# Attention block with a token-mixing MLP on one core: the last heads' repeated rows loaded first, half a row tile more in the last pair, no maximum tiles in the first iteration

## The chip, the cores and the metric

The kernel runs on one core of a Trainium2 chip. The metric is the device time of one execution in microseconds (us); a version of the kernel is given by the median of several executions. The engines of the core work side by side and are tied together by semaphores: TensorE (PE) multiplies matrices, VectorE (DVE) and ScalarE (ACT) do elementwise work and empty the accumulators (PSUM banks), GpSimd (POOL) helps with elementwise work, and the SP queue issues most loads and stores. ACT and POOL issue a few DMAs as well.

## What is computed

`x` is a sequence of 2048 tokens of width 640. Two branches read it, and a gate of each token mixes them:

```python
qkv = (x @ wqkv).reshape(B, S, 3, H, Dh).transpose(2, 0, 3, 1, 4)    # H = 32 heads of Dh = 20
q, k, v = qkv
p = softmax(einsum("bhqd,bhkd->bhqk", q, k) * Dh ** -0.5)
a = einsum("bhqk,bhkd->bhqd", p, v).transpose(0, 2, 1, 3).reshape(B, S, D) @ wo

h = layernorm(x)                                                     # over the channels
u = gelu(einsum("bsd,sf->bdf", h, w1) + b1)                          # F = 1728, over the tokens
b = (einsum("bdf,fs->bds", u, w2) + b2).transpose(0, 2, 1)

g = sigmoid((x * gate_w).sum(-1, keepdims=True))
out = g * a + (1 - g) * b
```

All of it is float32. The kernel keeps the accuracy by splitting operands into a high and a low part and multiplying three times (high x high, high x low, low x high).

## The kernel before

**Stages.** First come the projections to q, k and v, and the layer norm. Then comes the MLP, whose result, already weighted by 1 - g, is stored to DRAM as `y_d`. During the MLP the maxima that the softmax needs are computed for the first half of the head pairs. Then comes the attention loop, and behind it the product with `wo`, here called the tail.

**The attention loop** runs over 16 pairs of heads (`p`) and 32 iterations (`it`) in each: two halves of the queries by 16 tiles of keys. One iteration does this on PE: two score matmuls into a double bank (`st_pair`, one wide exponential on ACT), a third score matmul into a single bank (`st_one(g, 0)`), then up to two maximum tiles, a fourth score matmul (`st_one(g, 1)`), and eight `pv` matmuls of the iteration before, which need its exponentials. The single score tiles rotate over the banks `one0`, `one1` and `s3`. A *maximum tile* (`s_next`, line 213) is a score matmul into one of two `s` banks whose rows DVE reduces to their maxima (line 219); they are made ahead of their use, for later head pairs. `LEFT` of them are left for the loop, and `take` says how many an iteration does: two in each iteration but the very first, until they run out. That is in iteration 8 of the last pair. The very first iteration of the first pair has its scores made ahead, so the first one that computes scores is number 1.

**The last pair.** When the maximum tiles have run out, the `s` banks are free, and the last pair does part of the tail's work between its scores. `first_row` and `row_half` multiply the first row tile (128 tokens, the first 512 of 640 input channels) by `wo`, in two halves of 320 output columns; a pass is a pair of matmuls on 64 rows each (`pair64`, line 49), and a half has 12 passes. A half uses both `s` banks and is emptied by two DVE instructions that add it to the row of `y_d` loaded before (line 1057).

**What hangs on the last pv.** The output of the heads `o_d`, not yet divided by the sums `l_d`, goes through DRAM. For the early heads the reciprocals are repeated for each of the 20 channels of a head in `r_d`. For the last four heads that is done behind the loop: `last_load` loads their sums, `last_recip` takes the reciprocals on DVE and stores them to `rc_d` from ACT's queue, and `l_rest` loads each row of `rc_d` 20 times, into 20 partitions of the tile `rbl` (four DMAs of 160 KB, line 1011).

**The tail.** Its operands are loaded in two kinds of tiles. *e-tiles* (`e_load(q)`, q = 0 to 7) hold the first 512 channels for 256 tokens: 512 KB of `o_d` (`ore`) and 512 KB of reciprocals (`rbe`). The *l tile* (`l_load`) holds the last 128 channels for all tokens: 1 MB of `o_d` (`orl`), 384 KB of `r_d` for the heads before the last four (into partitions 0 to 47 of `rbl`), and the rows from `l_rest` in the others. `e_high` and `l_high` multiply output by reciprocal on DVE (line 978) and take the high part on ACT (line 980); `e_low` and `l_low` take the low part on DVE (line 986). Row tiles then go through `a_tile` (line 1142): tile t needs the e-tile t // 2, and for its last 128 channels the l tile. Tiles 1 to 7 do only the first 512 channels at first. Tiles 8 to 15 do all of them, and each is followed by the missing part of tile t - 8. The results rotate over four pairs of banks, and an evacuation on DVE (line 1148) adds each to the row of `y_d`; then it is stored.

**What sets the order.** In this part the order of every engine's instructions and of the SP queue is the order in which the program writes them. So a DMA on SP that waits holds up all that SP issues later, and a DVE instruction that waits for a load holds up the evacuations behind it. Before the change SP issues e4, l, e5, then the repeated rows, then e6 and e7. On DVE, the multiplication of e5 is written in tile 4's turn ahead of the evacuation of tile 4, that of l in tile 6's turn.

Of the kernel before, what the change touches and what calls it, by code (L numbers as in the profile page):

```python
# [7 lines left out]
F32 = mybir.dt.float32  # L8
F32R = mybir.dt.float32r
AF = mybir.ActivationFunctionType  # L10
OP = mybir.AluOpType
AX = mybir.AxisListType

P = 128
S, D, H, DH, F = 2048, 640, 32, 20, 1728
NP = H // 2
NT = S // P
NC = D // P
# [6 lines left out]
HALF = D // 2  # L25
# [6 lines left out]
def gated_mix(ctx, tc, xT, x, wqk, wv0, wv1, wo, w1, w1t, b1, w2, b2, out):  # L32
    nc = tc.nc
# [29 lines left out]
    o_d = dram.tile([D, S], F32, name="o_d")  # L63
# [8 lines left out]
    psum = ctx.enter_context(tc.tile_pool(name="psum", bufs=1, space=PSUM))  # L72
# [19 lines left out]
    def s_tile(shape, name):  # L92
        return psum.tile(shape, F32, tag="s", bufs=2, name=name)
# [22 lines left out]
    g_t = cp.tile([P, NT], F32, name="g_t")  # L116
# [324 lines left out]
    for half in range(2):  # L441
        wvh, wvl = wvs[half]
        width = HALF + 2 if half == 0 else HALF
        for t in range(NT):
            n = NT * half + t
# [11 lines left out]
            ps = one_tile([P, width], f"v{half}_{t}")  # L457
            q, cols = t // 4, slice((t % 4) * P, (t % 4 + 1) * P)
# [387 lines left out]
    ap = ctx.enter_context(tc.tile_pool(name="ap", bufs=1))  # L846
# [89 lines left out]
    woh = [ap.tile([P, D], F32R, name=f"woh{c}") for c in range(NC)]  # L936
# [8 lines left out]
    o_raw, o_hl, l_hl = {}, {}, {}  # L945
# [13 lines left out]
    tys = {}  # L959
# [28 lines left out]
    def e_load(q):  # L988
        o_load(q, slice(0, (NC - 1) * P), NC - 1, 256, "e", 2)
# [6 lines left out]

    L0 = (H - LAST) * DH - (NC - 1) * P

    def l_load():
        raw, rb = [ap.tile([P, 4, 512], F32, name=f"{n}l") for n in ("or", "rb")]  # L1000
        r0 = (NC - 1) * P
        nc.sync.dma_start(raw.rearrange("p a b -> p (a b)"), o_d[r0:])
        rb = rb.rearrange("p a b -> p (a b)")
        nc.sync.dma_start(rb[:L0], r_v[r0:r0 + L0])
        for q in range(4):
            o_raw[q, "l"] = raw[:, q:q + 1], rb[:, q * 512:(q + 1) * 512].unsqueeze(1)
        return rb

    def l_rest(rb):
        for h in range(LAST):  # L1010
            nc.sync.dma_start(rb[L0 + h * DH:L0 + (h + 1) * DH], rc_d[h:h + 1].broadcast_to([DH, S]))
# [24 lines left out]

    def st_one(g, j):
        n = (2 * g + j) % 3
        ps = psum.tile([P, 512], F32, tag=("one0", "one1", "s3")[n], bufs=1, name=f"st{g}_1{j}")
        st_mm(g, j, 1, ps)  # L1040
        pt = lp.tile([P, 512], F32, tag="pt", bufs=5, name=f"p{g}_1{j}")
        nc.scalar.activation(pt, ps, AF.Exp, scale=SCALE)  # L1042
        pts[g][j, 1] = pt

    row_mms, row_ps, row_evacs = [], [], []

    def row_half(c):
        row_ps[:] = [s_tile([P, HALF], f"a0_{c}_{k}") for k in range(2)]
        oh, ol = o_hl[0]
        cols = slice(c * HALF, (c + 1) * HALF)  # L1050
        passes = [e for k in range(NC - 1) for e in ((oh[:, k, :P], woh[k]), (oh[:, k, :P], wol[k]), (ol[:, k, :P], woh[k]))]
        for i, (a, b) in enumerate(passes):
            row_mms.append((list(row_ps), a, b[:, cols], i == 0, i == len(passes) - 1))

        def evac(ps=list(row_ps)):
            for k in range(2):
                nc.vector.scalar_tensor_tensor(tys[0][:, cols], ps[k], g_t[:, :1], tys[0][:, cols], op0=OP.mult, op1=OP.add)

        row_evacs.append(evac)

    def first_row(it):
        if it in (10, 21):
            row_half(it // 21)
        for _ in range(2 if it in (14, 18, 26) else 1):
            if row_mms:
                pair64(*row_mms.pop(0))
        if it == 19:
            row_evacs.pop(0)()

    LEFT = NP * 128 + 2 - S_AHEAD  # L1070
    for p in range(NP):
        qs = st_src[p][1]
        if 8 <= p < 8 + NC:
            load_wo(p - 8)
        for it in range(32):
            qh, kt = divmod(it, NT)
            if p + 1 < NP:
                if it == 6:
                    st_src[p + 1] = base_stack(p + 1, True)
                if it == 13:  # L1080
                    load_v(p + 1)
                if it == 27:
                    load_m(p + 1, st_src[p + 1][1], 0)
            if it == 12 and p:
                load_m(p, qs, 1)
            if it == 14 and due_stack:
                n = due_stack.pop()
                if n < NP:
                    s_src[n] = s_stack(n)
            if p == NP - 1:  # L1090
                if it in (0, 14, 18, 29):
                    e_load((0, 14, 18, 29).index(it))
                if 13 <= it < 13 + NT:
                    y_load(it - 13)
                if it in (5, 20, 25):
                    q = (5, 20, 25).index(it)
                    e_high(q, lp if q == 2 else ap, nc.gpsimd)
                    e_low(q, nc.gpsimd)
            if kt == 0:
                pv = psum.tile([P, 512], F32, tag="pv", bufs=1, name=f"pv{p}_{qh}")  # L1100
            take = min(LEFT - given, 2) if p or it else 0
            g = p * 32 + it
            if g:
                st_pair(g)
                if p == NP - 1:
                    first_row(it)
                st_one(g, 0)
            else:
                pts[0] = first_p
            for _ in range(take):  # L1110
                s_next()
            if g:
                st_one(g, 1)
            given += take
            if take and given == LEFT:
                s_finish()
            pv_flush()
            if p * 32 + it in later:
                later.pop(p * 32 + it)()
            pend.append((p, qh, kt, pv, pts.pop(p * 32 + it)))  # L1120
    def a_tile(t, cs):
        n = a_count[0] % 4
        a_count[0] += 1
        name = f"a{t}_{cs[0]}"
        if n == 0:
            two = psum.tile([P, 2, 512], F32, tag="two", bufs=1, name=name)
            ps = [two[:, i, :HALF] for i in range(2)]
        elif n == 2:
            ps = [s_tile([P, HALF], f"{name}_{i}") for i in range(2)]
        else:  # L1130
            ps = [psum.tile([P, HALF], F32, tag=tag, bufs=1, name=f"{name}_{tag}") for tag in (("one1", "one0") if n == 1 else ("s3", "pv"))]
        passes = []
        for k in cs:
            (oh, ol), n, i = (o_hl[t // 2], 2, k) if k < NC - 1 else (l_hl[t // 4], 4, 0)
            cc = slice((t % n) * P, (t % n + 1) * P)
            passes += [(oh[:, i, cc], woh[k]), (oh[:, i, cc], wol[k]), (ol[:, i, cc], woh[k])]
        mms = [(i, c) for i in range(len(passes)) for c in range(2)]
        if t == NT - 1:
            mms.sort(key=lambda e: e[1])
        for i, c in mms:  # L1140
            a, b = passes[i]
            nc.tensor.matmul(ps[c], a, b[:, c * HALF:(c + 1) * HALF], start=(i == 0),  # L1142
                             stop=(i == len(passes) - 1))

        def evac():
            c = slice(t, t + 1)
            for i in range(2):
                nc.vector.scalar_tensor_tensor(tys[t][:, i * HALF:(i + 1) * HALF], ps[i], g_t[:, c], tys[t][:, i * HALF:(i + 1) * HALF], op0=OP.mult, op1=OP.add)
                if t == NT - 1:
                    put = (nc.scalar if i else nc.sync).dma_start  # L1150
                    put(out[t * P:(t + 1) * P, i * HALF:(i + 1) * HALF], tys[t][:, i * HALF:(i + 1) * HALF])
            if t != NT - 1 and NC - 1 in cs:
                nc.sync.dma_start(out[t * P:(t + 1) * P, :], tys[t])

        return evac

    a_count = [0]
    assert not row_mms
    first = a_tile(1, range(NC - 1))
    row_evacs.pop(0)()  # L1160
    first()
    pv_flush()
    e_load(4)
    last_rb = l_load()
    e_high(3, lp)
    e_low(3)
    e_load(5)
    last_recip()
    l_rest(last_rb)
    for t in range(2, NT):  # L1170
        q = t // 2 + 3
        lates = {NT // 2 - 2: (2, 0), NT // 2 + 1: (3, 1)}.get(t, ())
        for n in lates:
            l_high(n)
        for n in lates:
            l_low(n)
        if t % 2 == 0 and q < NT // 2:
            e_high(q, ap if q % 4 < 2 else lp)
        evacs = [(t, range(NC) if t >= NT // 2 else range(NC - 1))]
        if t >= NT // 2:  # L1180
            evacs.append((t - NT // 2, [NC - 1]))
        if t == NT - 1:
            evacs.reverse()
        evacs = [a_tile(*e) for e in evacs]
        for f in evacs:
            f()
        if t % 2 == 0 and q < NT // 2:
            e_low(q)
            if q + 2 < NT // 2:
                e_load(q + 2)  # L1190
# [49 lines left out]
```

## Time and profile before

| | us |
|---|---|
| median of 3 runs (lowest to highest) | 1772.01 (1771.06 to 1773.87) |
| the profiled execution's own time | 1770.92 |
| its span, first to last instruction | 1769.1 |
| first scores of the loop to the last pv, about | 723.4 to 1698.5 |
| the tail behind it | 1698.5 to 1769.1 |
| PE busy | 1760.1 (99%) |
| ACT busy | 1482.0 (84%) |
| DVE busy | 1225.9 (69%) |
| POOL busy | 659.9 (37%) |

TensorE's granted clock was 1.00 in all of the span. A busy PE includes the time of pipelined matmuls, so two engines can both read as busy all the time while one of them sets the pace. In the profile's rows the first number is the start in us from the span's beginning, the second the length; what stands in square brackets is the idle time ahead of the instruction on its engine, and what ended it. `SPq` and `ACTq` are DMA issues of these queues. Names such as `st`, `pv`, `ore`, `rbl` are the program's tiles; the tiles of the row product are called `a`, `a_one`, `a_s` and `a_pv` after the banks that they use.

### The profile page before, as it was taken

How to read it: one execution, taken by the hardware profiler on the slowest of the kernel's cores; microseconds unless marked ns; L12 is line 12 of the kernel's file. 1: busy time of each engine (PE TensorE's matmuls, PEld its weight loads, DVE VectorE, ACT ScalarE, POOL GpSimd, SP SyncE). 2: the span in 40 equal slices, each digit the busy share in tenths (PEclk: the TensorE clock that was granted, in tenths of full speed). 3: DMA queues.
4: the chain of work that ended last, by engine and by line, in shares of the span. 5: the costliest groups of instructions: out<-in, count | busy, mean ns of one | idle time of the engine just before them, and what ended most of it. 6: DMA issues, size and time to landing. Idle time of an engine off the chain costs nothing.

```text
span 1769.1 us, 39556 instructions
## 1 busy us (share of the span) xinstructions
PE 1760.1 (99%) x15008; PEld 1091.6 (62%) x15008; DVE 1225.9 (69%) x2379; ACT 1482.0 (84%) x2565; POOL 659.9 (37%) x988
## 2 busy tenths in 40 slices
PE   9999999999999999999999999999999999999998
PEld 7998899999999999533333333333333333333378
DVE  5303289999999899776777676777777677767335
ACT  4354388888888886899999999999999999999930
POOL 2223577889877777111211111121322121211400
PEclk9999999999999999999999999999999999999999
DMA  8767876467675564434314234053353143301553
GB/s 304 248 196 252 266 184 172 142 176 208 179 200 144 156 187 138 101 63 110 65 41 86 49 73 94 10 114 67 49 140 73 43 94 66 73 19 45 195 136 137
DMA packets 155625, 225.20 MB, mean 127 GB/s; under 512 B 66548, under 2 KB 93572, under 8 KB 151752
## 3 DMA queue, kind: packets, MB, share of 16 engines
q1 hardware_dynamic: 136902, 193.14, 40.1%
q0 software_dynamic: 15648, 24.28, 5.8%
q10 hardware_dynamic: 2884, 5.25, 1.1%
q8 instruction: 118, 1.93, 0.5%
q14 instruction: 73, 0.60, 0.1%
HBM read 166.88 MB, written 55.36 MB: 126 GB/s over the span
## 4 chain that ended last, share of the span: by engine, by line
PE 97%; DMA 2%; DVE 1%; ACT 0%; issue 0%; SPq 0%; ACTq 0%; DVEq 0%
PE pv L931 29%; PE st L1027 23%; PE s L213 12%; PE y L49 10%; PE u L49 10%; PE qk L55 8%; PE v L55 4%; PE a_one L1142 1%; PE a L1142 1%; DMA rc_d<-rl_last 1%; DMA ore<-o_d 0%; PE a_pv L1142 0%; PE a_s L1142 0%; DMA k_d<-evh 0%; DMA wr<-in_wqk_dram 0%; PE a L49 0%
## 5 line engine op out<-in xcount | busy, mean ns | idle before, releaser
L219 DVE TENSOR_REDUCE mx<-s 128x1 f32<-128x512 f32 x1280 | 835.2, 687 | 280.9 <-PE s L213 143.7
L1042 ACT ACTIVATE p<-st 128x512 f32<-128x512 f32 x1022 | 563.4, 618 | 0.0
L931 PE MATMUL pv<-p,v 128*32 128x512 f32 x4088 | 545.3, 605 | 0.0
L1034 ACT ACTIVATE p<-st 128x1024 f32<-128x1024 f32 x511 | 532.7, 1042 | 1.5 <-PE st L1027 1.4
L1027 PEld LDWEIGHTS st<-qs_True,ks_True 62*128 62x128 f32 x2044 | 245.1, 185 | 433.8 <-ACT p L1034 425.9
L1027 PE MATMUL st<-qs_True,ks_True 62*128 62x512 f32 x2044 | 494.6, 446 | 0.1
L213 PE MATMUL s<-ks_False,qs_False 60*128 60x512 f32 x1152 | 325.1, 391 | 0.4 <-ACT ov L228 0.3
L44 POOL TENSOR_TENSOR wl<-wr,wh 128x512 fp32r<-128x512 f32 x228 | 275.5, 1220 | 62.5 <-ACT wh L41 49.1
L238 DVE CUSTOM_DVE_ANT_0 ov<-s,ov 128x512 f32<-128x512 f32 x384 | 264.1, 688 | 36.2 <-PE s L213 24.7
L213 PE MATMUL s<-sk,sq 60*128 60x512 f32 x896 | 281.6, 394 | 0.0
L228 ACT ACTIVATE ov<-s 128x512 f32<-128x512 f32 x384 | 228.8, 598 | 63.0 <-PE s L213 53.0
L912 POOL DMA_DIRECT2D l_d<-oev x124 | 60.7, 496 | 411.0 <-DVE oev L904 402.6
L49 PE MATMUL y<-gh,wh 64*128 64x320 f32 x896 | 198.2, 305 | 0.0
L213 PEld LDWEIGHTS s<-ks_False,qs_False 60*128 60x128 f32 x1152 | 194.5, 184 | 3.1 <-ACT ov L228 0.9
L931 PEld LDWEIGHTS pv<-p,v 128*32 128x32 f32 x4088 | 81.3, 108 | 186.1 <-issue 174.5
L49 PE MATMUL u<-hh,wh 64*128 64x320 f32 x864 | 192.9, 304 | 0.0
L49 PE MATMUL u<-hl,wh 64*128 64x320 f32 x864 | 192.8, 304 | 0.0
L49 PE MATMUL y<-gh,wl 64*128 64x320 f32 x832 | 191.8, 305 | 0.0
L49 PE MATMUL y<-gl,wh 64*128 64x320 f32 x832 | 191.6, 305 | 0.0
L49 PE MATMUL u<-hh,wl 64*128 64x320 f32 x800 | 180.9, 304 | 0.0
L41 ACT ACTIVATE wh<-wr 128x512 fp32r<-128x512 f32 (+3 forms) x247 | 146.9, 599 | 38.3 <-PE y L49 15.7
L213 PEld LDWEIGHTS s<-sk,sq 60*128 60x128 f32 x896 | 166.2, 186 | 15.2 <-DVE mx L219 0.4
(189 smaller groups left out, 2388.8 us busy)
## 6 DMA issues: line engine op xcount, KB each, us to landing
wr<-in_w_dram SPq DMA_DIRECT2D x192, 256.0 KB
ks_True<-k_d SPq DMA_DIRECT2D x96, 160.0 KB
qs_True<-q_d SPq DMA_DIRECT2D x192, 80.0 KB
qs_False<-q_d SPq DMA_DIRECT2D x96, 80.0 KB
v_d<-vt SPq DMA_DIRECT2D x32, 212.0 KB
sk<-k_d SPq DMA_DIRECT2D x42, 160.0 KB
sq<-q_d SPq DMA_DIRECT2D x84, 80.0 KB
v<-v_d SPq DMA_DIRECT2D x15, 424.0 KB
```

The costliest lines, as they stand in the source:

```text
L41: nc.scalar.activation(hi, src, AF.Copy)
L44: (lo_eng or nc.vector).tensor_sub(lo, src, hi.bitcast(F32))
L49: nc.tensor.matmul(ps[k], a[r], b[r], start=start, stop=stop)
L55: nc.tensor.matmul(ps, a, b, start=(i == 0 and k == 0), stop=(i == n - 1 and k == 2))
L213: nc.tensor.matmul(ps, qs[half][r, t * P:(t + 1) * P], ks[r, kc * 512:(kc + 1) * 512], start=True, stop=True)
L219: nc.vector.tensor_reduce(mx[:, slot, j, t: t + 1], ps, axis=AX.X, op=OP.max)
L228: nc.scalar.activation(over[j, kc], ps, AF.Relu)
L238: nc.vector.tensor_tensor_reduce(ov, ps, ov, 1.0, -3.0e38, OP.add, OP.max, mx[:, slot, j, t: t + 1])
L931: nc.tensor.matmul(pv[r: r + 32, :], v_tiles[p][:, kt, VW * j: VW * j + 32], pt[j, c], start=(kt == 0), stop=(kt == NT - 1))
L1027: nc.tensor.matmul(ps, ks[r, kt * P:(kt + 1) * P], qs[qh][r, c * 512:(c + 1) * 512], start=True, stop=True)
L1034: nc.scalar.activation(pt, ps, AF.Exp, scale=SCALE)
L1042: nc.scalar.activation(pt, ps, AF.Exp, scale=SCALE)
```

## The change

Three things are edited.

The loads of the tail: the l tile's buffers are made ahead without a load (`l_tiles`), the reciprocals and the four loads of repeated rows come directly behind e4, and the l tile's own loads and e5 come behind them. The multiplication of the first l tiles moves from tile 6's turn to tile 5's.

The row product in the last pair: three halves instead of two (row tile 0 whole, and the first 320 columns of row tile 1), begun in iterations 10, 18 and 26, with two passes in an iteration except in 15, 16, 23 and 24. Behind the loop only the other half of tile 1 is left, and the third half's evacuation.

The loop's first iteration does no maximum tiles, so all of them come one iteration later and the last two fall into iteration 9 of the last pair. The fourth score tile of that first iteration goes to an `s` bank instead of `one0`.

```diff
+    l_raw = []
+
+    def l_tiles():
+        raw, rb = l_raw[:] = [ap.tile([P, 4, 512], F32, name=f"{n}l") for n in ("or", "rb")]
+        for q in range(4):
+            o_raw[q, "l"] = raw[:, q:q + 1], rb[:, q:q + 1]
+        return rb.rearrange("p a b -> p (a b)")
+
     def l_load():
-        raw, rb = [ap.tile([P, 4, 512], F32, name=f"{n}l") for n in ("or", "rb")]
         r0 = (NC - 1) * P
-        nc.sync.dma_start(raw.rearrange("p a b -> p (a b)"), o_d[r0:])
-        rb = rb.rearrange("p a b -> p (a b)")
+        raw, rb = [t.rearrange("p a b -> p (a b)") for t in l_raw]
+        nc.sync.dma_start(raw, o_d[r0:])
         nc.sync.dma_start(rb[:L0], r_v[r0:r0 + L0])
-        for q in range(4):
-            o_raw[q, "l"] = raw[:, q:q + 1], rb[:, q * 512:(q + 1) * 512].unsqueeze(1)
-        return rb
...
     def st_one(g, j):
         n = (2 * g + j) % 3
-        ps = psum.tile([P, 512], F32, tag=("one0", "one1", "s3")[n], bufs=1, name=f"st{g}_1{j}")
+        if (g, j) == (1, 1):
+            ps = s_tile([P, 512], f"st{g}_1{j}")
+        else:
+            ps = psum.tile([P, 512], F32, tag=("one0", "one1", "s3")[n], bufs=1, name=f"st{g}_1{j}")
...
     def first_row(it):
-        if it in (10, 21):
-            row_half(it // 21)
-        for _ in range(2 if it in (14, 18, 26) else 1):
+        if it in (10, 18, 26):
+            n = (10, 18, 26).index(it)
+            row_half(n // 2, n % 2)
+        for _ in range(1 if it in (15, 16, 23, 24) else 2):
             if row_mms:
                 pair64(*row_mms.pop(0))
-        if it == 19:
+        if it in (16, 24):
             row_evacs.pop(0)()
...
-            take = min(LEFT - given, 2) if p or it else 0
+            take = min(LEFT - given, 2) if p or it > 1 else 0
...
-    first = a_tile(1, range(NC - 1))
+    first = a_tile(1, range(NC - 1), (1,))
     row_evacs.pop(0)()
     first()
     pv_flush()
     e_load(4)
-    last_rb = l_load()
+    last_rb = l_tiles()
     e_high(3, lp)
     e_low(3)
-    e_load(5)
     last_recip()
     l_rest(last_rb)
+    l_load()
+    e_load(5)
     for t in range(2, NT):
         q = t // 2 + 3
-        lates = {NT // 2 - 2: (2, 0), NT // 2 + 1: (3, 1)}.get(t, ())
+        lates = {NT // 2 - 3: (2, 0), NT // 2 + 1: (3, 1)}.get(t, ())
```

`row_half` now takes the row tile as well as the half, and `a_tile` takes the halves that it computes and empties.

More of the change, by code (lines that the diff above doesn't have):

```diff
@@ L1045, in gated_mix, with row_half @@
     row_mms, row_ps, row_evacs = [], [], []
-    def row_half(c):
-        row_ps[:] = [s_tile([P, HALF], f"a0_{c}_{k}") for k in range(2)]
+    def row_half(t, c):
+        row_ps[:] = [s_tile([P, HALF], f"a{t}_{c}_{k}") for k in range(2)]
         oh, ol = o_hl[0]
+        rows = slice(t * P, (t + 1) * P)
         cols = slice(c * HALF, (c + 1) * HALF)
-        passes = [e for k in range(NC - 1) for e in ((oh[:, k, :P], woh[k]), (oh[:, k, :P], wol[k]), (ol[:, k, :P], woh[k]))]
+        passes = [e for k in range(NC - 1) for e in ((oh[:, k, rows], woh[k]), (oh[:, k, rows], wol[k]), (ol[:, k, rows], woh[k]))]
         for i, (a, b) in enumerate(passes):
@@ L1056, in evac @@
             for k in range(2):
-                nc.vector.scalar_tensor_tensor(tys[0][:, cols], ps[k], g_t[:, :1], tys[0][:, cols], op0=OP.mult, op1=OP.add)
+                nc.vector.scalar_tensor_tensor(tys[t][:, cols], ps[k], g_t[:, t:t + 1], tys[t][:, cols], op0=OP.mult, op1=OP.add)
         row_evacs.append(evac)
     def first_row(it):
-        if it in (10, 21):
-            row_half(it // 21)
-        for _ in range(2 if it in (14, 18, 26) else 1):
+        if it in (10, 18, 26):
+            n = (10, 18, 26).index(it)
+            row_half(n // 2, n % 2)
+        for _ in range(1 if it in (15, 16, 23, 24) else 2):
             if row_mms:
                 pair64(*row_mms.pop(0))
-        if it == 19:
+        if it in (16, 24):
             row_evacs.pop(0)()
@@ L1120, in gated_mix, with a_tile @@
             pend.append((p, qh, kt, pv, pts.pop(p * 32 + it)))
-    def a_tile(t, cs):
+    def a_tile(t, cs, halves=(0, 1)):
         n = a_count[0] % 4
@@ L1136, in a_tile @@
             passes += [(oh[:, i, cc], woh[k]), (oh[:, i, cc], wol[k]), (ol[:, i, cc], woh[k])]
-        mms = [(i, c) for i in range(len(passes)) for c in range(2)]
+        mms = [(i, c) for i in range(len(passes)) for c in halves]
         if t == NT - 1:
@@ L1146, in evac @@
             c = slice(t, t + 1)
-            for i in range(2):
+            for i in halves:
                 nc.vector.scalar_tensor_tensor(tys[t][:, i * HALF:(i + 1) * HALF], ps[i], g_t[:, c], tys[t][:, i * HALF:(i + 1) * HALF], op0=OP.mult, op1=OP.add)
```

## Prediction

> **What bounds the kernel now.** I read the chain of waits first, by its shares and then in order of time, then the timelines of TensorE (PE), ScalarE (ACT), VectorE (DVE) and the SP queue around the three places that the diff touches: the start of the attention loop, its last pair, and the stage behind it. All times are of the profiled execution.
>
> The shares of the chain:
>
> ```profile
> PE 97%; DMA 2%; DVE 1%; ACT 0%; issue 0%; SPq 0%; ACTq 0%; DVEq 0%
> ```
>
> The end of the same chain (start, length, what ran):
>
> ```profile
> 1693.76 3.72 PE a L1142 x24
> 1697.48 1.07 PE pv L931 x8
> ...
> 1701.32 1.86 DMA rl_last<-l_d
> 1703.79 9.69 DMA rc_d<-rl_last
> ```
>
> The reader sees that PE sets the time nearly everywhere, and that the one long exception lies in the tail: 32 KB of reciprocals of the last heads need 9.69 us to reach DRAM, and their repeated rows (rbl) can be loaded only then. In the loop, PE and ACT both run without a gap at about 1.90 us an iteration, so small things decide there which of them is late.
>
> **First iteration without maximum tiles.** ACT's exponentials at the loop's start, and the two rows that made the second one late:
>
> ```profile
> 724.01 1.02 ACT L1034 ACTIVATE p<-st 128x1024 f32<-128x1024 f32 x1 [1.07 <-PE st L1027]
> 724.93 1.08 ACT L1042 ACTIVATE p<-st 128x512 f32<-128x512 f32 x2
> 726.33 1.03 ACT L1034 ACTIVATE p<-st 128x1024 f32<-128x1024 f32 x1 [0.32 <-PE st L1027]
> ...
> 728.23 1.02 ACT L1034 ACTIVATE p<-st 128x1024 f32<-128x1024 f32 x1
> ```
>
> ```profile
> 723.71 0.61 DVE L708 TENSOR_SCALAR ty<-y,omg,b2o 128x320 f32<-128x320 f32 x1 [3.64 <-PE y L49]
> ```
>
> ```profile
> 724.37 0.49 PE L1027 MATMUL st<-qs_True,ks_True 62*128 62x512 f32 x1
> ```
>
> The wide exponentials start 2.32 us apart, then 1.90: 0.42 us are lost once. The fourth score matmul (724.37) sat behind two maximum tiles and waited for DVE to empty bank one0 (723.71 + 0.61 = 724.32). The change takes away both: no maximum tiles, and this matmul writes to an s bank. At most 0.42 us is gained. But the next iteration's second maximum tile rotates onto that s bank and must wait for the exponential reading it, which ends at 724.93 + 1.08 = 726.0, about 0.4 us after PE would reach the tile; part of the gain goes back. I take **-0.2** (bounds -0.42 and 0). The two tiles reappear in iteration 9 of the last pair, which now has none. ACT sets the period there, so they cost nothing in themselves; but they leave ACT with no backlog for what follows.
>
> **Half a row tile more in the last pair.** PE with two row pairs in an iteration, then with one (starts of the first score matmuls of three iterations), and ACT's wide exponentials:
>
> ```profile
> 1659.55 0.50 PE L1027 MATMUL st<-qs_True,ks_True 62*128 62x512 f32 x2
> ...
> 1661.52 0.50 PE L1027 MATMUL st<-qs_True,ks_True 62*128 62x512 f32 x2
> ...
> 1663.34 0.51 PE L1027 MATMUL st<-qs_True,ks_True 62*128 62x512 f32 x2
> ```
>
> ```profile
> 1648.93 1.02 ACT L1034 ACTIVATE p<-st 128x1024 f32<-128x1024 f32 x1
> ...
> 1660.14 1.19 ACT L1034 ACTIVATE p<-st 128x1024 f32<-128x1024 f32 x1
> ...
> 1662.06 1.17 ACT L1034 ACTIVATE p<-st 128x1024 f32<-128x1024 f32 x1
> ...
> 1667.68 1.24 ACT L1034 ACTIVATE p<-st 128x1024 f32<-128x1024 f32 x1
> ```
>
> An iteration with two pairs takes PE 1.97 us (1661.52 - 1659.55), one with one pair 1.82. ACT's ends (start plus length) come every 1.90 us through both: 1661.33, 1663.23. What absorbs the 0.07 is ACT's backlog, seen as the length of the wide exponential: 1.02 with none, 1.24 full, so 0.22 us. Before, two-pair iterations stood alone (14, 18, 26) and cost nothing. Now there are sixteen, in runs 10-14, 18-22 and 26-31. The first run starts with no backlog and loses 5 x 0.07 = 0.35; iterations 15-17 restore about 0.2, so the second loses 0.15; the third 6 x 0.07 - 0.2 = 0.22. Sum **+0.7** (bounds: 0, if all is hidden as now; 16 x 0.07 + 0.1 = 1.2, if nothing is).
>
> In exchange the stage behind the loop loses half of its first tile: 24 matmuls took 3.72 us ahead of the last pv, and 12 remain: **-1.86** before the last pv, and so before all that hangs on it (the last sums, their reciprocals, rc_d). The last exponential is done by then, so nothing takes the place of these matmuls. Of the evacuations one moves behind the loop as before; DVE has room there.
>
> **The tail's loads in another order.** The SP queue, then DVE, then PE of that stage, then the DMA's rate in stretches (last two columns: busy share, GB/s):
>
> ```profile
> 1701.77 0.38 SPq L957 DMA_DIRECT2D ore<-o_d  x1
> ...
> 1703.12 0.34 SPq L1002 DMA_DIRECT2D orl<-o_d  x1
> ...
> 1703.98 1.00 SPq L957 DMA_DIRECT2D ore<-o_d  x1
> ...
> 1713.56 1.70 SPq L1011 DMA_DIRECT2D rbl<-rc_d  x4
> ```
>
> ```profile
> 1707.92 1.23 DVE L978 TENSOR_TENSOR ore<-ore,rbe 128x1024 f32<-128x1024 f32 x1 [4.17 <-DMA rbe<-r_d]
> ...
> 1717.61 1.23 DVE L978 TENSOR_TENSOR ore<-ore,rbe 128x1024 f32<-128x1024 f32 x1 [5.13 <-DMA rbe<-r_d]
> ...
> 1721.19 1.00 DVE L1148 SCALAR_TENSOR_TENSOR oy<-a,g_t,oy 128x320 f32<-128x320 f32 x2
> 1723.64 1.29 DVE L978 TENSOR_TENSOR orl<-orl,rbl 128x512 f32<-128x512 f32 x2 [1.45 <-DMA ore<-o_d]
> ...
> 1726.25 1.22 DVE L978 TENSOR_TENSOR ore<-ore,rbe 128x1024 f32<-128x1024 f32 x1
> 1727.38 1.00 DVE L1148 SCALAR_TENSOR_TENSOR oy<-a_one,g_t,oy 128x320 f32<-128x320 f32 x2
> ```
>
> ```profile
> 1719.62 0.31 PE L1142 MATMUL a_s<-woh,ohe 128*128 128x320 f32 x1
> ...
> 1725.05 0.41 PE L1142 MATMUL a_s<-woh,ohl 128*128 128x320 f32 x1 [1.60 <-ACT ohl L980]
> ...
> 1727.98 0.87 PE L1142 MATMUL a_one<-woh,ohe 128*128 128x320 f32 x2 [0.76 <-DVE oy L1148]
> ```
>
> ```profile
> 1703.00:1706.00 3.00, 3.00 (x23) 3.00 (x22) 0.55 (x1) 0.00 (x0) 0.00 (x0) 1.00 0.97 301
> ...
> 1716.00:1717.00 1.00, 1.00 (x9) 1.00 (x9) 0.00 (x0) 0.00 (x0) 0.00 (x0) 1.00 0.63 140
> 1716.00:1723.00 7.00, 7.00 (x48) 6.85 (x48) 4.29 (x6) 1.06 (x1) 0.00 (x0) 1.00 0.98 168
> 1723.00:1726.00 3.00, 1.40 (x9) 1.00 (x8) 2.26 (x4) 1.24 (x2) 0.00 (x0) 1.00 1.09 348
> ```
>
> Before, the DMA stream is e4 (1 MB, issued 1701.77), l (1.4 MB, 1703.12), e5 (1 MB, 1703.98), and only then the repeated rows (1713.56). e5 is multiplied at 1717.61, l and the repeated rows at 1723.64; PE is held up at 1725.05 and 1727.98 by this, about 2.8 us: 8.36 lie between the start of tile 8 (1719.62) and of tile 9 (1727.98), and the 36 matmuls between them take 36 x 3.72 / 24 = 5.6.
>
> After, SP issues e4, then stands at the repeated rows until rc_d has landed, and l, e5, e6 stand behind it on SP. But e5 is needed first: DVE multiplies e5 in tile 4's turn, and behind that multiply stand the evacuation of tile 4 (whose banks tile 8 uses), e5's low part, the l tiles (now one turn earlier), the evacuations of tiles 5 and 6, and e6. So **when e5 lands is what this edit moves**, and all is late by it.
>
> I work it out on the clock of before, with the last pv left where it was. e4 moves at 301 GB/s, so it is through at about 1706.5 and landed at 1707.92. rc_d, issued at 1703.79 behind e4, lands with it: 1707.9 (bounds 1705.65, with the 1.86 of the small load rl_last; 1708.9, a microsecond behind e4). First bytes of the repeated rows about 1.2 later, 1709.1: the DMA stands idle for about 2.6 us. The repeated rows are 4 x 160 KB; in the one stretch where they run nearly alone they move 140 GB/s, which is 4.7 us (bounds: 1.9 at 348 GB/s; 5.5, if one adds what 1716-1723 lost, 7 x (1 - 168 / 348) = 3.6). Then l and e5 need what they needed before, 1706.5 to 1717.61, 11.1 us. e5 lands at 1709.1 + 4.7 + 11.1 = **1724.9**, against 1717.61 (bounds 1719.9 and 1726.7). From there DVE needs 1721.19 - 1717.61 = 3.6 to the end of e5's low part, 2.6 for l (1723.64 to 1726.25), 0.9 for the evacuation of tile 5, 1.1 for e6 (1726.25 to 1727.38), and 0.6 until PE starts tile 9: 8.8 us. Tile 9 starts at 1733.7 instead of 1727.98: **+5.7** (bounds +0.7 and +7.5). From tile 9 on PE ran without a gap to the end, and the order of work there is the same.
>
> [...]
>
> **The sum.** -0.2 + 0.7 - 1.86 + 5.7 = **+4.3 us** (bounds -1.6 to +7.0, adding the ends with -1.86 fixed). On the profiled execution's own 1770.92 that is 1775.2; the median of the runs shown stands 1.09 above that execution, so 1776.3.
>
> **Rivals.** First, *rc_d is not held up by e4*: it interleaves and lands at 1705.65, the repeated rows move from 1706.85, and e5 lands at 1722.65: 2.25 less, 1774.0. For it speaks that rl_last took 1.86 us on an idle DMA; against it the 9.69 us that rc_d spent among other loads. [...]
>
> Second, *faster: the DMA runs at its full rate*. If rc_d lands early and the slow stretches (140 and 168 GB/s) come from the mixing of the repeated rows with other loads, which the new order ends, then the repeated rows, l and e5, 3.1 MB in all, go at 348 GB/s from 1706.85 on: 9.0 us and about 1.1 to land, 1717.0. Tile 9 starts at 1725.8, 2.2 early, and with -1.36 of the other terms this is -3.6: 1772.0 - 3.6 = 1768.4. The turn is at 1727.98 - 8.8 = 1719.2: an e5 that lands before it shortens the tail, a later one lengthens it; the whole change breaks even at 1720.5. For it: rc_d's 9.69 us are on the chain, and the change shortens them. Against it: the 140 GB/s stood in a stretch with hardly anything else in flight.
>
> Third, *the earlier row evacuation stalls the loop*. Its rows:
>
> ```profile
> 1665.35 0.69 DVE L904 COPY oev<-pv 128x512 f32<-128x512 f32 x1 [13.34 <-PE pv L931]
> 1669.83 1.21 DVE L1057 SCALAR_TENSOR_TENSOR oy<-a,g_t,oy 128x320 f32<-128x320 f32 x2 [3.78 <-DMA oy<-y_d]
> ```
>
> The evacuation moves from iteration 19 to 16 and on DVE ahead of the copy oev, for which PE's next pv waits. If the y row really landed only at 1669.83, as that label says, the copy would be 5.7 us late: 1782.0. I think the label names the wrong releaser, since that pass of the row ended on PE at that moment.
>
> Fourth, *no change*: gains and losses cancel, with e5 at about that 1720.5: 1772.
>
> **How the numbers follow.** The forecast with its own range (1774.5 to 1779) has 0.55, the interleaved rc_d 0.20, the full rate 0.11, the stalled loop 0.04, no change 0.10. A measurement of this kernel can tell 0.2%, 3.5 us, from no change. Slower by more: three quarters of the forecast, the stall, and a little of the first rival, 0.48. Faster by more: most of the second rival and the low tail of the fourth, 0.12. Within: 0.40. The range leaves out the stall and most of the full rate: 1769.5 to 1779.
>
> **What would show it.** On the profile after: the wide exponentials at the loop's start 1.9 apart at once, or 2.1 in the next iteration; PE's two-pair iterations at 1.97 with the wide exponential at 1.02 in iterations 11-14; 12 matmuls of 1.8 us ahead of the last pv; the first repeated-row issue about 4 us behind that of rc_d, and a hole in the DMA's rate ahead of it; the multiply of e5 7 us later after the last pv than now, and PE waiting at the start of tile 8, which it does not now. Wrong would be: e5 multiplied within 21.7 us of the last pv (it is 20.1 now), PE running from tile 7 to tile 9 without a wait, or a stall of pv in iteration 17.

## The result, and the profile after

| | median, us (lowest to highest) | ratio to before |
|---|---|---|
| before | 1770.85 (1769.43 to 1773.87, 11 runs) | |
| after | 1775.62 (1774.13 to 1779.07, 11 runs) | 1.0026 [1.0018, 1.0035] |

The change makes the kernel 4.8 us slower; +4.3 was forecast. The profiled execution took 1774.13 us, its span 1772.3 against 1769.1. The chain of waits of the kernel after, at the end of the loop and in the tail (start, length, what ran):

```profile
1693.44 1.96 PE a L1151 x12
1695.40 1.07 PE pv L931 x8
...
1709.69 13.78 DMA ore<-o_d
```

Twelve matmuls instead of 24 now stand ahead of the last pv, and it starts at 1695.40 instead of 1697.48. But the wait for rc_d that stood on the chain has been replaced by a longer wait for a load, 13.78 us. The chain puts it to the load issued at 1709.69, which is e6; DVE's own row and the order of issue say that it is e5. The SP queue of the kernel after:

```profile
1700.28 0.38 SPq L957 DMA_DIRECT2D ore<-o_d  x1
1700.71 0.49 SPq L957 DMA_DIRECT2D rbe<-r_d  x1
1705.55 1.41 SPq L1015 DMA_DIRECT2D rbl<-rc_d  x4
1707.30 0.35 SPq L1010 DMA_DIRECT2D orl<-o_d  x1
...
1708.99 0.59 SPq L957 DMA_DIRECT2D rbe<-r_d  x1
```

SP issues e4 (1700.28), then stands until rc_d has landed, and e5 is issued only at 1708.99, behind the repeated rows and the l tile. What DVE does with these loads, in order, and what that does to PE:

```profile
1705.49 1.23 DVE L978 TENSOR_TENSOR ore<-ore,rbe 128x1024 f32<-128x1024 f32 x1 [3.21 <-DMA rbe<-r_d]
...
1722.32 1.23 DVE L978 TENSOR_TENSOR ore<-ore,rbe 128x1024 f32<-128x1024 f32 x1 [12.28 <-DMA rbe<-r_d]
...
1725.90 1.29 DVE L978 TENSOR_TENSOR orl<-orl,rbl 128x512 f32<-128x512 f32 x2
...
1730.55 1.00 DVE L1157 SCALAR_TENSOR_TENSOR oy<-a_one,g_t,oy 128x320 f32<-128x320 f32 x2
```

```profile
1695.33 1.06 PE L931 MATMUL pv<-p,v 128*32 128x512 f32 x8
...
1724.16 0.61 PE L1151 MATMUL a_s<-woh,ohe 128*128 128x320 f32 x1 [6.45 <-DVE oy L1157]
...
1731.42 0.60 PE L1151 MATMUL a_one<-woh,ohe 128*128 128x320 f32 x2
```

DVE stands 12.28 us at e5's multiply, although the l tile, for whose sake the loads were put in this order, is multiplied without any wait behind it. The evacuation of tile 4 stands behind that multiply as well, and PE waits 6.45 us for it at the start of tile 8. From here on "behind the last pv" counts from the start of pv in PE's own rows (1697.41 before, 1695.33 after; the chain's rows start 0.07 later). e5 is multiplied 27.0 us behind the last pv (20.2 before), tile 9 starts 36.1 behind it (30.6 before).

What the DMA did meanwhile, in stretches of the kernel after (first column: from and to; the last three: granted TensorE clock, DMA busy share, GB/s):

```profile
1705.00:1706.00 1.00, 1.00 (x9) 1.00 (x8) 0.51 (x1) 0.00 (x0) 0.00 (x0) 1.00 0.00 0
1706.00:1707.00 1.00, 1.00 (x9) 1.00 (x8) 1.00 (x2) 0.20 (x1) 0.00 (x0) 1.00 0.49 82
...
1710.00:1713.00 3.00, 3.00 (x23) 3.00 (x21) 0.04 (x1) 0.00 (x0) 0.00 (x0) 1.00 0.98 131
...
1719.00:1722.00 3.00, 0.00 (x0) 0.00 (x0) 0.00 (x0) 0.00 (x0) 0.00 (x0) 0.90 1.09 348
1722.00:1728.00 6.00, 3.84 (x14) 3.76 (x15) 5.29 (x8) 2.29 (x3) 0.00 (x0) 0.50 0.46 143
```

There is the hole while SP waits for rc_d (nothing from 1705 to 1706, 82 GB/s behind it), then a long stretch that is mostly slow (131 from 1710 to 1713, 152 to 336 behind that), and 348 GB/s only from 1719 on.

### The profile page after: what moved, and what is told of

It reads as the page before. It is cut to its first block, busy times and chain, and to the rows that moved or that the text cites. A ratio compares the mean times of both kernels' runs of the same rounds, so it can differ in the third digit from the quotient of the medians.

```text
span 1772.3 us, 39583 instructions
## 1 busy us (share of the span) xinstructions
PE 1759.6 (99%) x15020; PEld 1092.3 (62%) x15020; DVE 1227.0 (69%) x2380; ACT 1482.1 (84%) x2565; POOL 658.8 (37%) x988
## 4 chain that ended last, share of the span: by engine, by line
PE 98%; DMA 1%; DVE 0%; ACT 0%; issue 0%; SPq 0%; POOL 0%; ACTq 0%; DVEq 0%
PE pv L931 29%; PE st L1031 22%; PE s L213 12%; PE y L49 10%; PE u L49 10%; PE qk L55 8%; PE v L55 4%; PE a_one L1151 1%; DMA ore<-o_d 1%; PE a L1151 1%; PE a_s L1151 1%; PE a_pv L1151 1%; PE a L49 0%; DMA wr<-in_wqk_dram 0%; DMA rbe<-r_d 0%; DVE mx L219 0%
## 5 line engine op out<-in xcount | busy, mean ns | idle before, releaser
L49 PE MATMUL u<-hh,wh 64*128 64x320 f32 x864 | 188.8, 305 | 0.0
L49 PE MATMUL u<-hl,wh 64*128 64x320 f32 x864 | 188.7, 305 | 0.0
L49 PE MATMUL u<-hh,wl 64*128 64x320 f32 x800 | 177.3, 305 | 0.0
```

The costliest lines, as they stand in the source:

```text
L49: nc.tensor.matmul(ps[k], a[r], b[r], start=start, stop=stop)
```

## The experiments

**The two halves of the change.** One kernel keeps the row product and the loop's start of the change, but has the loads and the multiply of l in their old order:

```diff
     last_rb = l_tiles()
+    l_load()
     e_high(3, lp)
     e_low(3)
+    e_load(5)
     last_recip()
     l_rest(last_rb)
-    l_load()
-    e_load(5)
...
-        lates = {NT // 2 - 3: (2, 0), NT // 2 + 1: (3, 1)}.get(t, ())
+        lates = {NT // 2 - 2: (2, 0), NT // 2 + 1: (3, 1)}.get(t, ())
```

> The changed kernel with the tail's loads in their old order (e4, l, e5, repeated rows) and the l multiply back in tile 6's turn; the loop's start and the row tiles as changed. If the loads' order is what costs (my theory), the loop's part stands alone: -0.2 at the start, +0.7 in the last pair, -1.86 behind it, so about 1.3 us below the kernel before, and e5 multiplied about 20 us behind the last pv. If the runs of two-pair iterations are what costs (rival), it stays 3 us or more above the kernel before.

The other is the kernel before with only the new order of loads (and the multiply of l in tile 5's turn):

> The kernel before with the new order of the tail's loads and the earlier l multiply alone. My theory: about 5.3 to 5.7 us above the kernel before, with e5 multiplied about 27 us behind the last pv and PE idle at the start of tile 8 for some 6 us. The rival, by which the loop's part costs: within 1 us of the kernel before.

Measured: old loads 1769.89 us, 0.9990 [0.9982, 0.9999] of before; new loads only 1777.29, 1.0032 [1.0019, 1.0044], against a before of 1771.59 in the same comparison. That is -1.7 and +5.7, together +4.0, of the +4.8 of the whole. PE's waits in the tail of the first, and the one of the second:

```profile
1719.21 0.39 PE L1151 MATMUL a_s<-woh,ohe 128*128 128x320 f32 x1 [0.46 <-DVE oy L1157]
1726.26 0.88 PE L1151 MATMUL a_one<-woh,ohe 128*128 128x320 f32 x2 [0.77 <-DVE oy L1157]
```

```profile
1725.02 0.60 PE L1146 MATMUL a_s<-woh,ohe 128*128 128x320 f32 x1 [5.45 <-DVE oy L1152]
```

So the loss is that of the load order (with the earlier multiply of l), and the rest of the change is a small gain, whose interval only just excludes no change. In the second kernel e5 is multiplied 26.0 us behind the last pv (1723.19 - 1697.20), 1.0 less than in the change, which has the same order of loads: single executions differ that much.

**Whether it is e5's multiply that holds up PE.** Here the changed order of loads stays, and DVE and ACT do what they do in another order: the multiply of e5, which stood ahead of the evacuation of tile 4, and its low part, which stood behind it, both come behind the evacuation of tile 6 (e6 and e7 correspondingly later, and the load of e7 with them).

```diff
-        if t % 2 == 0 and q < NT // 2:
-            e_high(q, ap if q % 4 < 2 else lp)
+        if t == 2:
+            e_high(4, ap)
...
-        if t % 2 == 0 and q < NT // 2:
-            e_low(q)
-            if q + 2 < NT // 2:
-                e_load(q + 2)
+        if t == 2:
+            e_low(4)
+            e_load(6)
+        if t in (6, 8, 10):
+            e_high(t // 2 + 2, ap if (t // 2 + 2) % 4 < 2 else lp)
+            e_low(t // 2 + 2)
+            if t == 6:
+                e_load(7)
```

> The changed kernel, with the multiplies of e5, e6 and e7 written behind the evacuations of tiles 6, 8 and 10 in place of ahead of those of tiles 4, 6 and 8; the loads' order stays. If the new order costs only because DVE stands at e5's multiply with the evacuations behind it (my theory), PE goes through tiles 4 to 9 with under 1 us of waiting, tile 9 starts about 28 us behind the last pv instead of 36, and the kernel is about 8 us faster than the changed one, 3 below the one before. If instead the l rows or tile 10's own need of e5 come too late (rival), a wait moves there, and less than half of the 8 us is won.

Measured: 1770.74, 0.9993 [0.9985, 1.0002]: 5.8 us less than the change by the two ratios (1.0026 - 0.9993, times 1771), less than the 8 that the theory expected. The wait at tile 8 is gone, and two smaller ones stand elsewhere. The first two rows are DVE's, the others PE's:

```profile
1720.80 1.29 DVE L978 TENSOR_TENSOR orl<-orl,rbl 128x512 f32<-128x512 f32 x2 [8.60 <-DMA rbl<-r_d]
...
1723.40 1.00 DVE L1157 SCALAR_TENSOR_TENSOR oy<-a,g_t,oy 128x320 f32<-128x320 f32 x2
```

```profile
1724.55 0.53 PE L1151 MATMUL a<-woh,ohl 128*128 128x320 f32 x2 [1.05 <-DVE oy L1157]
...
1738.36 0.88 PE L1151 MATMUL a_one<-woh,ohe 128*128 128x320 f32 x2 [2.13 <-DVE oy L1157]
```

Now the l tile's multiply is the first on DVE to wait for a load, with the evacuation of tile 5 (1723.40) behind it; PE waits 1.05 us for that, and 2.13 at tile 11 for another evacuation that stands behind later multiplies.

**All multiplies behind the evacuations that PE needs.** This version moves l's first multiply too, behind the evacuation of tile 7, and e5, e6, e7 behind l. Everything else is the change.

```diff
-        lates = {NT // 2 - 3: (2, 0), NT // 2 + 1: (3, 1)}.get(t, ())
-        for n in lates:
-            l_high(n)
-        for n in lates:
-            l_low(n)
-        if t % 2 == 0 and q < NT // 2:
-            e_high(q, ap if q % 4 < 2 else lp)
+        lates = {NT // 2 - 1: (2, 0), NT // 2 + 1: (3, 1)}.get(t, ())
+        if t == 2:
+            e_high(4, ap)
...
-        if t % 2 == 0 and q < NT // 2:
-            e_low(q)
-            if q + 2 < NT // 2:
-                e_load(q + 2)
+        if t == 2:
+            e_low(4)
+            e_load(6)
+        for n in lates:
+            l_high(n)
+        for n in lates:
+            l_low(n)
+        if t in (7, 9, 10):
+            m = {7: 5, 9: 6, 10: 7}[t]
+            e_high(m, ap if m % 4 < 2 else lp)
+        if t in (8, 9, 10):
+            e_low(t - 3)
+            if t == 8:
+                e_load(7)
```

> The changed kernel, its loads' order kept, with DVE's order in the tail rewritten so that no evacuation stands behind a multiply whose load is late: the l multiplies of tiles 8 and 0 and that of e5 behind the evacuation of tile 7, e5's low part behind tile 8's, e6 and the other l multiplies behind those of tiles 9 and 1, e7 behind those of tiles 10 and 2. In the run that moved only the e multiplies, PE still waited 1.1 us behind the l multiply (ahead of tile 5's evacuation) and 2.1 behind e6 and l (ahead of tile 9's). If the evacuations' place on DVE is the whole price (my theory), PE goes from the last pv to the end with under 0.5 us of waiting, and the time is 4 us below the kernel before. If the DMA itself is the bound (rival), tile 8 waits for the l tile's high part and the gain over that run is under 1 us.

The same DVE order on the kernel with the old loads:

> The same order on DVE, but with the loads in the order of the kernel before (e4, l, e5, repeated rows). There the repeated rows land last, about 25.5 us behind the last pv, and tile 8 wants the l tile's high part at about 25.7, which needs another 1.4: my theory expects one wait of 1 to 1.5 us at tile 8's last channels, and a time 2.5 to 3 us below the kernel before, so 1 to 1.5 behind the run with the new order. If the order of the loads makes no difference once DVE is free (rival), both come out within 0.5 us.

Measured: with the new loads 1766.11, 0.9973 [0.9963, 0.9982]; with the old loads 1769.23, 0.9989 [0.9980, 0.9998], before being 1771.65 here. DVE's two multiplies in the first:

```profile
1719.35 1.29 DVE L978 TENSOR_TENSOR orl<-orl,rbl 128x512 f32<-128x512 f32 x2
...
1722.05 1.23 DVE L978 TENSOR_TENSOR ore<-ore,rbe 128x1024 f32<-128x1024 f32 x1
```

and l's multiply in the second (DVE), with what it makes PE wait for:

```profile
1721.99 1.29 DVE L978 TENSOR_TENSOR orl<-orl,rbl 128x512 f32<-128x512 f32 x2 [2.67 <-DMA ore<-o_d]
```

```profile
1723.40 0.42 PE L1151 MATMUL a_s<-woh,ohl 128*128 128x320 f32 x1 [1.46 <-ACT ohl L980]
```

With the new loads neither multiply waits, and PE has no wait at all from the last pv to the end. e5 is multiplied 26.0 us behind the last pv, hardly earlier than the 27.0 of the change, and it does no harm there. With the old loads the one wait left, 1.46 us, is for the l tile. The label on l's multiply names the load of an e-tile, which that multiply does not read; of what it does read, the repeated rows are issued last (1711.98), so I take the wait to be for them, the wait that the new order takes away. So the new load order is worth something, but only with the DVE order that belongs to it. By the ratios this version is 4.8 us faster than before and 9.4 faster than the change. The medians of the two versions lie 3.1 us apart, their profiled executions 1.9 (1766.10 and 1767.95), and the one wait is 1.46; where the rest comes from stays open.

**What makes e5 late: the wait for rc_d, or the bytes ahead of it?** In three variants of the change the repeated rows do not wait for rc_d: they are read from r_d, where rows of other heads lie ready. So the last four heads are divided by the sums of other heads, and nothing else differs. The first reads one row 20 times, as the change does; the second reads 20 different rows; the third reads all 80 rows with one DMA instead of four.

```diff
-            nc.sync.dma_start(rb[L0 + h * DH:L0 + (h + 1) * DH], rc_d[h:h + 1].broadcast_to([DH, S]))
+            nc.sync.dma_start(rb[L0 + h * DH:L0 + (h + 1) * DH], r_v[h * DH:h * DH + 1].broadcast_to([DH, S]))
```

```diff
-            nc.sync.dma_start(rb[L0 + h * DH:L0 + (h + 1) * DH], rc_d[h:h + 1].broadcast_to([DH, S]))
+            nc.sync.dma_start(rb[L0 + h * DH:L0 + (h + 1) * DH], r_v[h * DH:(h + 1) * DH])
```

```diff
-        for h in range(LAST):
-            nc.sync.dma_start(rb[L0 + h * DH:L0 + (h + 1) * DH], rc_d[h:h + 1].broadcast_to([DH, S]))
+        nc.sync.dma_start(rb[L0:], r_v[:LAST * DH])
```

> The changed kernel, but the repeated rows are read from reciprocals of earlier heads, stored long before, so that SP does not wait for rc_d: the division of the last four heads is by other heads' sums. The bytes and their order are the same. My theory splits e5's delay into an idle gap of 1 to 2.6 us and the repeated rows' own bytes ahead of it, 4.7: so e5 comes 1 to 2.6 us earlier and the kernel is that much faster than the changed one, still 2 us or more above the one before. If the wait for rc_d is the whole price (rival), it comes down to the kernel before or below it.

> As the run that reads the repeated rows from other heads' reciprocals, but each of the 20 partitions reads its own copy of the row in DRAM in place of 20 reads of one row: same bytes, same destination, other addresses. If the slow stretch (130 to 160 GB/s) comes from the 20 partitions that are written (my theory), e5 is multiplied at the same distance from the last pv as there, about 25 us, within 0.7. If it comes from reading one row 20 times (rival), that is 2 us or more shorter.

> The changed kernel, with the four loads of 20 repeated rows each replaced by one load of 80 rows of r_d (640 KB as before, into the same 80 partitions, no wait for rc_d; the last four heads are so divided by the sums of other heads, and the output differs there). The kernel that read 4 x 20 rows of r_d multiplied e5 25.6 us behind the last pv. If the narrowness of each load (20 rows, 20 partitions) is what makes the stretch slow, 640 KB go at the rate of wide loads, about 340 GB/s and 1.9 us instead of 4.7 at 140 GB/s: e5 is multiplied about 22.8 behind the last pv. If only the bytes ahead of e5 count, or the slow rate belongs to the DRAM rows read, it stays at 25.6.

A fourth keeps the wait and splits each load of 20 rows into one of 16 and one of 4:

```diff
-            nc.sync.dma_start(rb[L0 + h * DH:L0 + (h + 1) * DH], rc_d[h:h + 1].broadcast_to([DH, S]))
+            for d0, d1 in ((0, 16), (16, DH)):
+                nc.sync.dma_start(rb[L0 + h * DH + d0:L0 + h * DH + d1], rc_d[h:h + 1].broadcast_to([d1 - d0, S]))
```

> The changed kernel, each load of 20 repeated rows split into one of 16 rows and one of 4 (eight DMAs, the same bytes and partitions, the same wait for rc_d). If the rate is limited by the number of DMA engines that a load of 20 rows gets, the loads of 16 rows go faster, and e5 is multiplied 1 us or more earlier than the 27.0 behind the last pv of the changed kernel. If it is limited by the few partitions written at a time, it stays at 27.0 or gets later, as the loads of four rows write still fewer.

e5's multiply in these four, one fence for each, in that order:

```profile
1720.92 1.23 DVE L978 TENSOR_TENSOR ore<-ore,rbe 128x1024 f32<-128x1024 f32 x1 [9.89 <-DMA rbe<-r_d]
```

```profile
1721.62 1.23 DVE L978 TENSOR_TENSOR ore<-ore,rbe 128x1024 f32<-128x1024 f32 x1 [10.13 <-DMA rbe<-r_d]
```

```profile
1719.03 1.23 DVE L978 TENSOR_TENSOR ore<-ore,rbe 128x1024 f32<-128x1024 f32 x1 [8.19 <-DMA rbe<-r_d]
```

```profile
1727.07 1.23 DVE L978 TENSOR_TENSOR ore<-ore,rbe 128x1024 f32<-128x1024 f32 x1 [15.76 <-DMA rbe<-r_d]
```

| | e5 multiplied behind the last pv | PE's wait at tile 8 | time |
|---|---|---|---|
| the change | 27.0 | 6.45 | 1775.62, ratio 1.0026 |
| rows from r_d, one row 20 times | 25.0 | 4.46 | 1774.21, ratio 1.0015 [1.0006, 1.0024] |
| rows from r_d, 20 rows | 25.6 | 5.08 | 1773.51 (one run) |
| rows from r_d, 80 rows in one DMA | 23.8 | 3.22 | 1770.49 (one run) |
| rows from rc_d, 16 + 4 rows | 30.2 | 9.63 | 1778.76 (one run) |

The kernel before was at 1771.65 in the comparison of the third row, and at 1770.56, in one run, in that of the last two. The distances are each from one execution, so differences under about 1 us say little.

The two variants with four loads of r_d were meant to take the wait for rc_d away, but they only move it. The chain of the first:

```profile
1702.73 11.36 DMA rc_d<-rl_last
...
1714.10 0.37 SPq L957
```

SP issues the repeated rows, l and e5's first load by 1706.45, but then stands 7.3 us at e5's second load until rc_d has landed, and issues it at 1714.10, later than the change does (1708.99). In the second variant it stands 6.1 us. So the gain that was expected of the first (1 to 2.6 us) came out, but not for the reason given. Why this load waits for rc_d, which it does not read, is not shown. In the program it is the eighth DMA behind rc_d, as e5's first load is the eighth behind e4's second, and that one went out at 1706.45, when e4 had just landed (e4's multiply starts at 1706.48).

With one load of 80 rows e5's second load is the fifth behind rc_d, and it is issued at 1703.60, without any such wait. There e5 comes 3.2 us earlier than in the change (27.0 - 23.8), and the kernel takes as long as before (1770.49 against 1770.56). The other 3.6 of the 6.8 us by which the change delays e5 (23.8 - 20.2) stay: the repeated rows still run ahead of e5. How the 3.2 divide between the wait and the four narrow loads stays open, as this variant takes both away. Reading one row 20 times costs nothing more than reading 20 rows (25.0 and 25.6).

The split into 16 and 4 makes it 3.2 us worse. Part of this may again be SP, which stands 2.9 us ahead of e5's two loads, by the profile until earlier ones of the split loads have landed, and issues the second at 1714.45. The first case of the expectation, loads of 16 rows that go faster, does not show: from 1707 to 1710, before the next load is issued at 1710.27, the split rows move 131 to 148 GB/s (DMA busy share 0.37 to 0.89), about the 140 of the 20-row loads in the kernel before (0.63). That the few partitions written at a time limit the rate, the second case, is not shown by this either. Against it as the whole of the cause stands a stretch of the last variant:

```profile
1714.00:1717.00 3.00, 3.00 (x22) 3.00 (x22) 0.00 (x0) 0.00 (x0) 0.00 (x0) 1.00 1.01 131
```

131 GB/s in 3 us are 393 KB, 48 packets of 8 KB. From 1707 on 96 such packets had gone before them, and the repeated rows are only 80. So, if the packets ran in the order of issue, which is an assumption here, these are in the main rows of the next load, `o_d` for the l tile, which goes into all 128 partitions: it is slow too. From 1718 to 1719 the rate is 418 GB/s. In the kernel after, the stretch of 131 GB/s from 1710 to 1713 holds packets 79 to 126, so there too that load runs slowly. Why it does stays open.

**The loop's start.** The change without its `s` bank for the fourth score tile of the first iteration:

```diff
-        if (g, j) == (1, 1):
+        if False:
             ps = s_tile([P, 512], f"st{g}_1{j}")
         else:
```

> The changed kernel with the fourth score tile of the first iteration back in bank one0. It then waits for DVE to empty one0, as in the kernel before, but has no maximum tiles ahead of it and gives no s bank away. My theory: the second wide exponential starts about 2.3 us behind the first, 0.4 later than with the s bank, and the third 1.9 behind that, so that the sum over the two is 4.2, as before the change, and the 0.2 of the loop's start are gone. If the wait for the s bank is what costs (rival), the sum is 3.9 or less.

ACT's wide exponentials of the kernel after, and a maximum tile (PE) of its second iteration; then ACT of this variant and its fourth score tile (PE):

```profile
723.23 1.02 ACT L1038 ACTIVATE p<-st 128x1024 f32<-128x1024 f32 x1 [1.06 <-PE st L1031]
...
725.10 1.05 ACT L1038 ACTIVATE p<-st 128x1024 f32<-128x1024 f32 x1
...
727.25 1.02 ACT L1038 ACTIVATE p<-st 128x1024 f32<-128x1024 f32 x1
```

```profile
725.29 0.49 PE L213 MATMUL s<-ks_False,qs_False 60*128 60x512 f32 x1 [0.24 <-ACT p L1049]
```

```profile
724.06 1.02 ACT L1038 ACTIVATE p<-st 128x1024 f32<-128x1024 f32 x1 [1.07 <-PE st L1031]
...
726.37 1.02 ACT L1038 ACTIVATE p<-st 128x1024 f32<-128x1024 f32 x1 [0.31 <-PE st L1031]
...
728.28 1.02 ACT L1038 ACTIVATE p<-st 128x1024 f32<-128x1024 f32 x1
```

```profile
724.41 0.49 PE L1031 MATMUL st<-qs_True,ks_True 62*128 62x512 f32 x1 [0.31 <-DVE ty L708]
```

After, the first two distances are 1.87 + 2.15 = 4.02; before they were 2.32 + 1.90 = 4.22. Without the `s` bank they are 2.31 + 1.91 = 4.22 again, though the maximum tiles stay away: the fourth score tile waits for DVE to empty `one0` in any case. So the gain of 0.2 needs the bank, and leaving out the maximum tiles does nothing by itself. The variant's time, 1775.50 (one run), is that of the change.

## Why the prediction held

**The terms, one by one.** The start of the loop: -0.20 (predicted -0.2), with the give-back at the second maximum tile that the prediction described. The two-pair runs: from the first wide exponential of the loop to the last, 968.32 us before (724.01 to 1692.33) and 968.72 after (723.23 to 1691.95), +0.40. With the -0.20 of the start inside it, the rest of the loop costs +0.60. In the last pair alone, from its iteration 8 on, it is +0.74 (1648.93 to 1692.33 before, 1647.81 to 1691.95 after; predicted +0.7); the other 0.14 were gained little by little in the many iterations between, which no term claims. The last wide exponential before, and then rows of ACT after, from ahead of the first run, from the run itself, from the single iterations behind it and from the loop's end:

```profile
1692.33 1.25 ACT L1034 ACTIVATE p<-st 128x1024 f32<-128x1024 f32 x1
```

```profile
1647.81 1.02 ACT L1038 ACTIVATE p<-st 128x1024 f32<-128x1024 f32 x1
...
1651.61 1.02 ACT L1038 ACTIVATE p<-st 128x1024 f32<-128x1024 f32 x1
1653.56 1.02 ACT L1038 ACTIVATE p<-st 128x1024 f32<-128x1024 f32 x1
...
1661.39 1.02 ACT L1038 ACTIVATE p<-st 128x1024 f32<-128x1024 f32 x1
...
1668.87 1.13 ACT L1038 ACTIVATE p<-st 128x1024 f32<-128x1024 f32 x1
...
1691.95 1.02 ACT L1038 ACTIVATE p<-st 128x1024 f32<-128x1024 f32 x1
```

1.95 to 1.96 apart with no backlog (length 1.02), then the backlog builds up (1.13), and at the loop's end it is used up again. The half tile: from the last wide exponential to the last pv 5.08 before (1692.33 to 1697.41) and 3.38 after (1691.95 to 1695.33), -1.70 (predicted -1.86; the 12 matmuls take 1.96 and not half of 3.72). The tail: from the last pv's start to the end of the span 71.69 before and 76.97 after, +5.28, and to the start of tile 9 +5.5 (predicted +5.7). The sum of what was measured, -0.20 + 0.60 - 1.70 + 5.28, is +3.98 in the profiled executions; their spans differ by 3.2 because the work ahead of the loop took 0.78 less in this one (the first wide exponential at 723.23 instead of 724.01), which none of the terms claims. The medians differ by 4.8: the profiled execution of the kernel after is the fastest of its 11. Single executions differ by about 1 us, as said above, so that the terms meet the forecast more closely than that is luck. The upper end of the range adds up to +6.8 (0 + 1.2 - 1.86 + 7.5), not +7.0.

**The tail's steps.** They came out right as a sum, with errors that cancelled. From the last pv to the issue of rc_d 6.91 us (1695.40 to 1702.31), 0.6 more than before, as SP could issue the small load of the sums only 4.43 behind the last pv instead of 3.84; the prediction kept that distance. From there to the repeated rows' issue 3.24 (1705.55), where 4.1 was taken. From there to e5's multiply 16.77, where 1.2 + 4.7 + 11.1 = 17.0 was taken: the first packet of the repeated rows ran 0.9 behind their issue (no row was given for the 1.2), and from it, at 1706.4, to the multiply 15.9 passed, where 4.7 + 11.1 = 15.8 was taken. Then 9.10 from the multiply to tile 9, where 8.8 was taken. The hole, with no packet from 1705.0 to 1706.4, was 1.4 us and not 2.6. The two terms for the bytes came out as a sum only: that the repeated rows by themselves take 4.7 is not shown, as part of the l tile's load ran in the same slow stretch.

**The rivals.** That rc_d interleaves with e4 fell. The DMA queues of the kernel after in the 1.7 us behind rc_d's issue, and in the 1.1 us behind those (packets, MB, share of the 16 engines; q10 is ACT's queue with rc_d, q1 SP's):

```profile
q1 hardware_dynamic: 624, 0.62, 105.5%
```

```profile
q1 hardware_dynamic: 185, 0.17, 45.9%
q10 hardware_dynamic: 144, 0.03, 14.0%
```

Not one packet of rc_d ran before 1704.0; all went as e4's ran out, and rc_d landed when e4 did (e4's multiply starts at 1705.49, the repeated rows are issued at 1705.55). The 3.24 us from its issue lie between the rival's 1.86 and the 4.1 taken. In the kernel before the two queues did run side by side, behind e4: from 1708 to 1710 SP's queue ran 99 packets (0.73 MB, most of them of 8 KB), and rc_d's queue 90 small ones (0.02 MB). That the large packets between are what made rc_d's 32 KB take 9.69 us there is a guess. The full rate fell too: e5's multiply, 27.0 behind the last pv, lies far beyond the 21.7 named as the turn, and the run with one load, at 23.8 without a wait for rc_d, shows that an early rc_d would not have been enough. The stalled loop fell: DVE's row evacuation and the copy oev ran back to back, at 1663.40 and 1664.63, and the three pv around them start 1.90 and 1.97 apart (1663.47, 1665.37 and 1667.34). "No change" is excluded by the interval.

The break-even rule held within about 1 us as long as the DVE order is the program's. The tail was to break even with e5 at 21.7 behind the last pv, the whole change at 23.0 (1720.5 - 1697.48). In the order of the table above, the change and its four variants have e5 4.0, 2.0, 2.6, 0.8 and 7.2 us beyond 23.0, and by their times they are 4.8, 2.6, 1.9, -0.1 and 8.2 us slower than the kernel before (the last three from single runs). The rule's premise, that the evacuations stand behind the multiply, is what the reordered version takes away: there e5 comes at 26.0 and PE never waits.

## What to carry to other kernels

When a load is moved ahead of another on an in-order queue, look at which of the two has its consumer first on the consuming engine, and at what else stands behind that consumer: here the multiply of the load that was pushed back had PE's evacuations behind it. Move the consumers with the loads (0.9973 instead of 1.0026), and put work that waits for a load behind the work that frees accumulators. Price a load by the rate that its own shape shows in the trace (140 GB/s for the repeated rows before), not by the 348 of other loads, and expect that a load behind it may be slowed as well (131 GB/s from 1710 to 1713 in the kernel after). When a variant is to take a wait away, look in its own trace whether the wait has gone or only moved: here SP stood 7.3 us at a later load of the same queue instead.

## What was not expected of the hardware

**The clock after a wait.** In and behind PE's 6.45 us without work (1717.7 to 1724.16) the granted clock was 0.50, from 1722 to 1728 (the windows row above). Two of tile 8's matmuls of the kernel after, and two later ones:

```profile
1725.23 0.47 PE L1151 MATMUL a_pv<-wol,ohe 128*128 128x320 f32 x1
1725.49 0.47 PE L1151 MATMUL a_s<-woh,ole 128*128 128x320 f32 x1
...
1729.08 0.31 PE L1151 MATMUL a_s<-wol,ohe 128*128 128x320 f32 x1
1729.22 0.31 PE L1151 MATMUL a_pv<-wol,ohe 128*128 128x320 f32 x1
```

They start 0.26 apart instead of 0.14, so this wait cost more than itself. Behind the waits of 3.22, 4.46, 5.08, 5.45 and 9.63 us matmuls of tile 8 start 0.26 to 0.27 apart as well (behind that of 3.22 only from 1722.11 on, 1.25 behind tile 8's start; the clock there is 0.50 from 1722 to 1725). In the run with the waits of 1.05 and 2.13 the clock was 1.00 from 1717 to 1738, with the first wait in it, and 29 matmuls behind the second took 4.52 us, 0.16 each. In the kernel after the slow clock cost little: 9.10 instead of 8.8 us from e5's multiply to tile 9, as tile 9 could not have started before the evacuation of tile 6 (from 1730.55) in any case.
